# A fused linear-attention and soft-MoE kernel: loads cut into 256 KB pieces with a limit on what is under way, and a new written-out order

## The chip, the cores and the metric

The kernel runs on one core of a Trainium2 chip. Five engines have queues of their own: TensorE (PE, with its weight loads as PEld), VectorE (DVE), ScalarE (ACT), GpSimd (POOL) and SyncE (SP), which here only issues DMAs. The metric is the device time of one execution in microseconds (us), as the median of several runs.

## The reference, cut to what matters

```
# gated linear attention, 4 batches x 8 heads, 768 positions, 48 channels
scale = min(|a|, 0.999) / (|a| + 1e-6);  a = a * scale           # complex a = a_re + i a_im
for t in range(768):                                             # S: 48 x 48 per head
    S_re, S_im = a_t * (S_re + i S_im) + k_t v_t^T (real part only)
    y_t = q_t . S_re
x = y as 3072 tokens x 384
# soft mixture of experts, 8 experts x 4 slots
logits = x @ phi;  d = softmax over tokens;  c = softmax over slots
slot_out[e] = relu((d^T x)[e] @ w1[e]) @ w2[e]                   # w1, w2: 12.6 MB each
out = c @ slot_out
```

## The kernel before, in words

The recurrence is turned into 128-position blocks. Work is cut into units u = 0 to 6 of up to four (batch, block) pairs; unit 0 and unit 6 hold two pairs. For each unit the gates `ar`, `ai` (real and imaginary part, 768 KB each for a whole unit) are loaded, turned into the logarithm of the size (`gates`, tasks `g`) and into a phase (`arctan`, tasks `t`); TensorE sums them along the block (`phase`, tasks `p`, tile `up`; `logs`, tasks `e`, tile `lp`); sines and cosines (`wave`, `w`) and exponentials scale q and k (`mults`, `h`). The third part of the channels is moved inside SBUF by DMAs into the tile `hm` (`mixed`, `M`). Then for each pair come the scores (`c`, tile `qd`), the transposes (`x`), the state update (`D`), the attention output (`a`) and its transpose (`f`), and for each finished block the soft-MoE running sums (`l`, `s`). After the last block the slots are merged (`me`, `si`), the hidden layer (`hd`, `tn`), the second layer (`ex`) and the outputs (`er`, `ou`, `mi`) follow.

What runs when is written out by hand. Every task is a Python generator; the string `ORDER` names the tasks, and each word runs one task up to its next `yield`. A star on a word sets `moe.other`, which moves that step to the other engine that can do it (ACT instead of DVE, POOL instead of DVE, and so on). `_InOrder.pin` fixes the order so traced on every engine. For tasks whose names begin with `la`, `q`, `v` or `w_` (the loads of gates, q and k, v, and weights) it also makes each DMA wait for the last TensorE instruction traced so far:

```python
HELD = ("la", "q", "v", "w_")
if held and isinstance(ins, mybir.InstDMACopy) and pe in self.last:
    self.after(ins, self.last[pe])
```

All DMAs go out on SP's queue, in the order of `ORDER`, so a DMA that waits holds up all that are behind it. The weights of the two layers come in 24 pieces `w_0` to `w_23` of 1 MB (128 x 2048 floats). Pieces 0 to 4 have tiles of their own (`wx`) and may be loaded at any time; the others take over tiles that the attention part has finished with (`hm`, `vt`, `we`, `qe2`, `wf`, `q01`, `e01`, and `wx` again). The tiles `ar`, `ai` have one buffer each, so the gates of the next unit are loaded when the last use of this unit's is over. Warm-up matmuls (`zz`) keep TensorE busy where the order expects it to be idle. At the end each of the 18 output tiles is copied out of PSUM by ACT or DVE (`result`) and stored by a DMA from SP. A check of the value ranges (`gd`) ends in a branch to a slow fallback, which is not taken here.

Of the kernel before, what the change touches and what calls it, by code (L numbers as in the profile page):

```python
# [11 lines left out]
F32 = mybir.dt.float32  # L12
# [31 lines left out]
HELD = ("la", "q", "v", "w_")  # L44

# [36 lines left out]
class _Moe:  # L82
# [219 lines left out]
    L0 g0 g0 g1 g0 g1 g0* q1.1 g1 g0 g1 g1 g0 g1 g0 g1 g0 g1 T0 t0 e0.2 e0.0 e0.2 e0.0 t1 L1 e0.2 e0.1 e0.2 e0.0 la1 h0.2 p0.1  # L302
    p0.1* p0.0 e0.0 p0.2 la1 p0.2 p0.1 e0.1* k0 w_3 v1 p0.0* w_0 p0.2 p0.0 w0.2* e0.1 k0 g2 g2 e0.1 T1 w0.2 h0.0 w0.0 w0.0 zz6 zz5
    k0 g2* zz14 zz13 w0.2 zz3 g2* h0.1 h0.2 M0 k0* h0.2 w0.0 h0.1 h0.0 t2 zz10 p1.2 M0 L2 g2 h0.0 w_2 zz9 g2 p1.2 p1.0 p1.1 p1.2
    h0.1 q1.2 p1.0 zz0 p1.1 c0.0 g2 g2 p1.0 w1.2* p1.1 e1.2 e1.2 c0.0* T2 w1.2 q1.0 w1.2 e1.0 e1.0 w1.0 e1.1 la2 L3 e1.2 e1.2 e1.1
    a0.0 e1.0 e1.0 a0.0 la2 h1.2 x0.0 c0.1 e1.1 x0.0 e1.1 x0.0 zz4 h1.0 h1.2 x0.1 h1.1 M1 x0.1* q2.0 c0.1* g3 g3 T3 w1.0 a0.1
    h1.2* f0.0 w1.0 x0.1* zz12 zz1 g3* k1 a0.1* k1 f0.0 h1.0 M1 g3 k1* h1.1 t3 h1.0 q2.1 f0.1 D0.1 D0.0 p2.2 L4 g3 p2.2 h1.1 D0.0*
    w_1 q2.2 c0.2 D0.1 f0.1 g3 p2.0 c0.2 p2.2 g3 p2.0* w2.2 p2.1 T4 w2.2 v2 c0.3 a0.2 g3 p2.1* w2.2 c0.3 e2.2 p2.0 e2.2 e2.1 L5
    e2.2 e2.0 e2.2 a0.2* la3 p2.1 a0.3 f0.2 e2.1 w2.0 e2.0 la3 h2.2 e2.1 e2.1 a0.3 h2.1 e2.0 f0.2* h2.2 x0.2 x0.2* c1.0 c1.0* e2.0
    x0.2 l0 g4 g4 h2.2* l0 f0.3 f0.3 D0.2 T5 w2.0 w2.0 l0 a1.0 h2.0 l0 x0.3 x0.3 c1.1 M2 g4* D0.2 x1.0 M2 a1.0* x0.3 k2 f1.0 c1.1*  # L310
    k2 x1.0 D0.3 h2.1* g4 a1.1 x1.0* f1.0 k2* x1.1 h2.0 h2.0 t4 a1.1 D0.3* h2.1* q3.0 x1.1* q3.2 p3.2 p3.2* p3.0 x1.1* L6 g4 D1.0
# [27 lines left out]
class _InOrder:  # L339


    def __init__(self, tc):
        self.tc, self.last = tc, {}
# [11 lines left out]

    def pin(self, held=False):
# [182 lines left out]
def _polar(ctx, tc, cst, phi_sb, bad, aa, qk, vv, phi, w1, w2, consts, out):  # L539
# [44 lines left out]

    def load_a(u):
# [393 lines left out]
    er = {}  # L979
# [195 lines left out]
```

## Time and profile before

| | |
|---|---|
| median of 3 runs | 269.23 us (268.44 to 271.13) |
| the profiled execution's own time | 268.24 us |
| its span in the trace | 266.7 us |
| busy: PE, DVE, ACT, POOL | 226.7, 192.0, 185.2, 69.1 us |
| mean share of the 16 DMA engines on SP's queue | 65.3% |
| granted TensorE clock, mean | 0.963 of full speed |

Busy time is summed over a whole span with unlike stages, so it is read by stretch: in the first some 50 us the first units are prepared, then TensorE works nearly without a gap through the attention, and from about 200 us on the weights stream in beside the merge and the two layers. The profiled execution is 1 us below the median of the runs.

### The profile page before, as it was taken

Reading aid. Unit: us, or ns where it says so; the run is one execution under the profiler, and the core shown is the slowest. Engines: PE = TensorE matmul, PEld = TensorE weight load, DVE = VectorE, ACT = ScalarE, POOL = GpSimd, SP = SyncE. Lnnn points to the kernel's source line nnn. Section 1 sums busy time; section 2 is a strip of 40 time slices with the busy share of each in tenths; the row PEclk is TensorE's granted clock in tenths of the full one; section 3 lists DMA queues with packets and bytes.
Section 4 is the critical chain, followed back from the end, with each engine's and each line's share of the span. In section 5 each row is a group of like instructions: output and inputs, shape, how many; then the busy total and the mean of one; then the engine's idle time right before and its main releaser. Section 6 shows DMA issues by size and latency. Waiting matters only on the chain.

```text
span 266.7 us, 10855 instructions
## 1 busy us (share of the span) xinstructions
PE 226.7 (85%) x4828; PEld 180.5 (68%) x4828; DVE 192.0 (72%) x341; ACT 185.2 (69%) x293; POOL 69.1 (26%) x89
## 2 busy tenths in 40 slices
PE   0572976699969999999997999999969897999980
PEld 0431865588848998799885998888867663249640
DVE  4479679799938899798998898976461146575660
ACT  4979598999867898997886989698932232234230
POOL 0000004212562218512663043534830121000000
PEclk9998699989979999999999999999998999999997
DMA  6788748945830828355365565448769397979886
GB/s 172 263 300 369 236 137 298 273 167 199 294 104 7 290 77 305 85 179 223 120 200 132 201 222 161 128 132 310 265 193 366 129 413 284 375 285 394 341 297 215
DMA packets 16389, 60.95 MB, mean 228 GB/s; under 512 B 1872, under 2 KB 5200, under 8 KB 13264
## 3 DMA queue, kind: packets, MB, share of 16 engines
q1 hardware_dynamic: 16336, 60.18, 65.3%
q8 instruction: 40, 0.66, 1.0%
q14 instruction: 13, 0.11, 0.1%
HBM read 49.17 MB, written 4.72 MB: 202 GB/s over the span
## 4 chain that ended last, share of the span: by engine, by line
PE 63%; ACT 10%; DVE 9%; DMA 8%; issue 6%; POOL 1%; SPq 0%; DVEq 0%; ACTq 0%
PE qd L834 10%; PE qd L884 7%; PE up L712 7%; PE qd L890 6%; DMA ai<-in_aa_dram 5%; PE op L257 4%; PE db L863 4%; PE hp L227 4%; PE lp L712 4%; PE tp L819 3%; PE xp L898 3%; DVE ai L662 2%; PE up L710 2%; PE o L293 2%; DMA ar<-in_aa_dram 1%
## 5 line engine op out<-in xcount | busy, mean ns | idle before, releaser
L712 PE MATMUL lp<-cst,ar 128*128 128x128 f32 x144 | 20.9, 290 | 11.5 <-DVE ar L677 11.5
L712 PEld LDWEIGHTS lp<-cst,ar 128*128 128x128 f32 x144 | 20.0, 203 | 12.5 <-DVE ar L677 12.0
L884 PE MATMUL qd<-scT,vt 128*48 128x128 f32 x352 | 24.6, 283 | 2.1 <-DVE scT L846 2.0
L712 PE MATMUL up<-cst,ai 128*128 128x128 f32 x144 | 23.3, 312 | 2.2 <-ACT ai L682 1.9
L712 PEld LDWEIGHTS up<-cst,ai 128*128 128x128 f32 x144 | 22.5, 226 | 3.9 <-ACT ai L682 2.4
L846 DVE TENSOR_TENSOR scT<-qd,cst 128x1024 f32<-128x1024 f32 x16 | 19.4, 1215 | 5.9 <-ACT yT L103 4.5
L834 PE MATMUL qd<-e 32*128 32x128 f32 x384 | 22.8, 298 | 0.0
L884 PEld LDWEIGHTS qd<-scT,vt 128*48 128x48 f32 x352 | 18.8, 125 | 5.7 <-DVE scT L846 2.9
L834 PE MATMUL qd<-q 32*128 32x128 f32 x416 | 21.4, 276 | 1.3 <-issue 1.3
L729 POOL COPY cr<-fc 128x4 f32<-128x4 f32 x15 | 4.2, 283 | 67.1 <-DVE fc L727 66.9
L779 POOL TENSOR_TENSOR qe<-qe,fc 128x512 f32<-128x512 f32 (+1 forms) x14 | 17.3, 1261 | 15.6 <-DVE qe L781 10.7
L576 ACT ACT_TABLE_LOAD x15 | 19.2, 1283 | 1.3 <-PEq L1158 1.0
L834 PEld LDWEIGHTS qd<-e 32*128 32x128 f32 x384 | 16.1, 188 | 3.9 <-issue 2.4
L834 PE MATMUL qd<-hm 32*128 32x128 f32 x352 | 18.1, 273 | 0.4 <-issue 0.4
L834 PEld LDWEIGHTS qd<-q 32*128 32x128 f32 x416 | 17.0, 189 | 1.8 <-issue 1.6
L579 ACT ACT_TABLE_LOAD x14 | 18.0, 1283 | 0.3
L849 POOL TENSOR_SCALAR_AFFINE_SELECT scT<-scT 128x1024 f32<-128x1024 f32 x8 | 8.8, 1098 | 35.4 <-ACT scT L848 35.4
L898 PE MATMUL xp<-cst,yT 128*128 128x128 f32 x96 | 15.0, 283 | 2.4 <-DVE yT L105 2.2
L662 DVE TENSOR_TENSOR ai<-ai,gt 128x384 f32<-128x384 f32 x22 | 13.2, 659 | 5.1 <-DMA ai<-in_aa_dram 3.9
L779 POOL TENSOR_TENSOR q<-q,fc 128x512 f32<-128x512 f32 (+1 forms) x12 | 14.5, 1228 | 9.2 <-DVE e L781 5.8
L103 ACT COPY yT<-qd 128x512 f32<-128x512 f32 x13 | 7.7, 591 | 12.8 <-PE qd L890 10.2
L863 PE MATMUL db<-vt,kt 128*32 128x48 f32 x960 | 13.9, 211 | 1.7 <-DVE tk L105 1.7
(199 smaller groups left out, 612.3 us busy)
## 6 DMA issues: line engine op xcount, KB each, us to landing
wx<-in_w_dram SPq DMA_DIRECT2D x10, 1024.0 KB, 6.4
q<-in_qk_dram SPq DMA_DIRECT2D x10, 512.0 KB, 5.6
hm<-qe SPq DMA_DIRECT2D x20, 256.0 KB, 4.7
ar<-in_aa_dram SPq DMA_DIRECT2D x5, 768.0 KB, 4.3
ai<-in_aa_dram SPq DMA_DIRECT2D x5, 768.0 KB, 6.6
vt<-in_vv_dram SPq DMA_DIRECT2D x5, 768.0 KB, 5.7
hm<-in_w_dram SPq DMA_DIRECT2D x3, 1024.0 KB, 6.9
we<-in_w_dram SPq DMA_DIRECT2D x3, 1024.0 KB, 5.5
```

The costliest lines, as they stand in the source:

```text
L227: self.nc.tensor.matmul(out=hp[x][32 * g : 32 * g + 32, :], lhsT=zs[hi][:, c, g, :], rhs=w1_chunk(12 * hi + 4 * c + g)[:, x * 512 : (x + 1 ...
L576: ACT.preload_act_table_set(LNEXP)
L579: ACT.preload_act_table_set(TRIG)
L662: (DVE if moe.other else POOL).tensor_tensor(out=i[:, b], in0=i[:, b], in1=t[:, b], op=ALU.mult)
L712: PE.matmul(out=out[:, b], lhsT=gate[:, b, P * j : P * j + P], rhs=tri, start=not u, stop=not u or b == b1 - 1)
L779: POOL.tensor_tensor(out=out[:, w], in0=in0[:, w], in1=in1[:, w], op=ALU.mult)
L834: PE.matmul(out=qd[:, i, P * g : P * g + P], lhsT=feat(u, g, c, 1, b)[r], rhs=feat(u, g, c, 0, b)[r], start=c == 0, stop=c == 2,)
L846: DVE.tensor_tensor(out=t, in0=sc, in1=mask.unsqueeze(1).unsqueeze(1).broadcast_to([P, 4, 2, P]), op=ALU.mult)
L863: PE.matmul(out=db[o, 3 * g + c], lhsT=kt[u, b][:, g, c, o], rhs=vt[u][:, b - _span(u)[0], 4 * g + i], start=True, stop=True)
L884: PE.matmul(out=o(g, i), lhsT=vt[u][:, b - _span(u)[0], 4 * g + i], rhs=scT[u, b][:, i, g], start=True, stop=not s)
L890: PE.matmul(out=o(g, i), lhsT=st[s - 1, b][r, 3 * g + c], rhs=feat(u, g, c, 0, b)[r], start=False, stop=c == 2)
L898: PE.transpose(out=xp[:, i].rearrange("p g d -> p (g d)"), in_=yT[s, b][:, i], identity=ident)
```

## The change

Loads that are issued before the 13th weight piece in the order are cut into column pieces of at most 256 KB (`PIECE`), by the function `load`. Each such load then also waits, on SP, for an earlier load to have landed, so that the bytes of itself and of those before it that may still be under way come to no more than 1.3 MB (`paced`); the DMAs of `mixed` count too. The first DMA above 512 KB (the first of the weight pieces 12 to 23 in the order, which stay whole) switches this off for good. `ORDER` is replaced as a whole: the same tasks in another sequence, with other stars. Two loads of weights stand in the early part instead of three, and they are `w_1` and `w_2`. Of the last third of the outputs, a tile that ACT copies is stored by a DMA from ACT's queue instead of SP's. The range check `gd`, which was over before the last outputs, is moved in among them. The rest of the diff splits tile creation from use (`third`) and drops an unused second definition.

```diff
+PIECE = 1 << 18
+UNDER_WAY = 1300000
+PACED = 12
...
-    def result(self, er, sr, n, os_, out):
+    def result(self, er, sr, n, os_, out, last=False):
...
-        self.copy(out=t, in_=o, by_act=n % 2 == 1)
+        by_act = n % 2 == 1
+        act = by_act != self.other
+        self.copy(out=t, in_=o, by_act=by_act)
         yield "mi2"
-        self.store.dma_start(out=out[:, n], in_=t)
+        (nc.scalar if act and last else self.store).dma_start(out=out[:, n], in_=t)
...
-    p0.1* p0.0 e0.0 p0.2 la1 p0.2 p0.1 e0.1* k0 w_3 v1 p0.0* w_0 p0.2 p0.0 w0.2* e0.1 k0 g2 g2 e0.1 T1 w0.2 h0.0 w0.0 w0.0 zz6 zz5
+    e0.0 e0.1 p0.2 p0.0 p0.0 h0.0* p0.2* g2 g2 p0.1* p0.2 w0.2 p0.0 h0.2 la1 w_1 e0.1 T1 w0.2 w0.2 p0.1 w0.0 k0 q1.0 w_2 w0.0 w0.0
...
-    ou2 bh mi2.0 mi2.5 mi2.0 mi2.0 mi2.1 mi2.3 mi2.5 mi2.2 mi2.3* mi2.3 mi2.2 mi2.1 mi2.4 mi2.1 mi2.5 mi2.4 mi2.4 mi2.2
+    mi2.2* mi2.2 mi2.4* mi2.5 mi2.4 mi2.3 mi2.1* zz7 gd mi2.3 mi2.5* gd mi2.1 mi2.5 gd mi2.0 gd mi2.0* mi2.0
...
+    def paced(self, ins):
+
+        size = n = 4 * math.prod(c for _, c in ins.outs[0].ap)
+        if self.sent is None or size > 2 * PIECE:
+            self.sent = None
+            return
+        for s, name in reversed(self.sent):
+            n += s
+            if n > UNDER_WAY:
+                self.after(ins, name)
+                break
+        self.sent.append((size, ins.name))
...
+            if isinstance(ins, mybir.InstDMACopy) and ins.engine == self.tc.nc.sync.engine:
+                self.paced(ins)
...
+    def load(out, in_):
+        if len(out.shape) == 4 and 4 * math.prod(out.shape) > PIECE:
+            for w in range(out.shape[1]):
+                load(out[:, w], in_[:, w])
+            return
+        if 4 * math.prod(out.shape) <= PIECE:
+            SP.dma_start(out=out, in_=in_)
+            return
+        if len(out.shape) == 3:
+            out, in_ = out.rearrange("p b x -> p (b x)"), in_.rearrange("p b x -> p (b x)")
+        n = out.shape[1]
+        w = -(-n // -(-4 * P * n // PIECE))
+        for x in range(0, n, w):
+            SP.dma_start(out=out[:, x : min(x + w, n)], in_=in_[:, x : min(x + w, n)])
...
-        SP.dma_start(out=wsl[x], in_=w1[x] if x < NW1 else w2[x - NW1])
+        src = w1[x] if x < NW1 else w2[x - NW1]
+        if x < PACED:
+            load(wsl[x], src)
+        else:
+            SP.dma_start(out=wsl[x], in_=src)
```

Line numbers of the changed kernel are 3 to 40 higher than those of the kernel before for the same statement.

First place: ACT, while the gates of unit 1 are prepared. The rows with `gt` and `ar` are the steps of `gates` (the last one, on `ar`, is the exponential whose result the sums `lp` wait for), those with `n` belong to `phase`. Before:

```order
L682 ACTIVATE ai<-ai 128x1536
L576 ACT_TABLE_LOAD
L671 ACTIVATE gt<-gt 128x1536
L724 ACTIVATE n<-up 128x512 x3
L675 ACTIVATE gt,esum<-ar 128x1536
L741 ACTIVATE fc_284<-fc_284 128x512
L579 ACT_TABLE_LOAD
L745 ACTIVATE fc_284<-fc_284 128x512
```

The same place in the changed kernel:

```order
L715 ACTIVATE ai<-ai 128x1536
L596 ACT_TABLE_LOAD
L704 ACTIVATE gt<-gt 128x1536
L757 ACTIVATE n<-up 128x512
L708 ACTIVATE gt,esum<-ar 128x1536
L757 ACTIVATE n<-up 128x512 x2
L599 ACT_TABLE_LOAD
L778 ACTIVATE fc_275<-fc_275 128x512
```

The exponential has moved ahead of the second and third `n`, and the absolute value on ACT (`fc`, line 741 before) has gone to DVE.

Second place: SP, from the gates of unit 1 to those of unit 2 (`wx` is a weight piece, `hm` the copies inside SBUF of unit 0). Before:

```order
L610 DMA q_131<-in_qk_dram 128x1024
L589 DMA ar<-in_aa_dram 128x1536
L591 DMA ai<-in_aa_dram 128x1536
L969 DMA wx<-in_w_dram 128x2048
L620 DMA vt<-in_vv_dram 128x1536
L969 DMA wx<-in_w_dram 128x2048
L806 DMA hm<-qe_114 64x2x256 x4
L969 DMA wx<-in_w_dram 128x2048
L610 DMA qe_288<-in_qk_dram 128x1024
L610 DMA q_131<-in_qk_dram 128x1024
L589 DMA ar<-in_aa_dram 128x1536
```

The same stretch in the changed kernel:

```order
L611 DMA q_129<-in_qk_dram 128x512 x2
L618 DMA ar<-in_aa_dram 128x512 x3
L618 DMA ai<-in_aa_dram 128x512 x3
L618 DMA wx<-in_w_dram 128x512 x4
L611 DMA q_129<-in_qk_dram 128x512 x2
L618 DMA wx<-in_w_dram 128x512 x4
L839 DMA hm<-qe_114 64x2x256 x4
L618 DMA vt<-in_vv_dram 128x512 x3
L611 DMA qe_312<-in_qk_dram 128x512 x2
L618 DMA ar<-in_aa_dram 128x512 x3
```

Ahead of the `hm` copies stand two weight pieces and half a load of q and k, now in ten pieces; a third weight piece behind them is gone, and v has moved behind the copies.

Third place: DVE in unit 5, where the four products of `ai` (task `g6`) and the copy of the carry `tk` (task `k4`) stand. Before:

```order
L781 TENSOR_TENSOR qe_1613<-qe_1613,fc_1718 128x1024
L662 TENSOR_TENSOR ai<-ai,gt 128x384 x4
L105 COPY tk<-ctp 128x128
L846 TENSOR_TENSOR scT<-qd,cst 128x1024
L867 TENSOR_TENSOR st<-db,st 128x288
```

On ACT in the changed kernel, where the copy of `tk` is now (the row with `tsum` is the step that reads the products of `ai`):

```order
L106 COPY d<-mt 128x128
L106 COPY xs<-xp 128x4x2x48
L106 COPY yT<-qd 128x512
L106 COPY tk<-ctp 128x128
L702 ACTIVATE gt,tsum<-ai 128x1536
```

The copy of `tk` no longer stands behind the four products of `ai` in its queue.

## Rows read from the trace of the kernel before

**Rows 1.** Busy time by stretch, with granted clock, DMA share and rate.

```profile
core 0: us, PE busy (x) PEld busy (x) DVE busy (x) ACT busy (x) POOL busy (x), PEclk, DMA share, GB/s
10.00:54.00 44.00, 31.20 (x348) 23.94 (x349) 33.30 (x59) 37.78 (x53) 5.14 (x9) 0.90 0.75 257
54.00:200.00 146.00, 139.15 (x3454) 120.46 (x3455) 122.03 (x179) 122.14 (x186) 60.14 (x71) 0.98 0.56 182
```

**Rows 2.** What PE waited for, 54 to 200 us: total, times, longest.

```profile
PE qd L890 <- issue: 2.5, 1, 2.5
PE tp L819 <- DVE q L781: 2.0, 1, 2.0
PE db L863 <- DVE tk L105: 1.7, 1, 1.7
```

**Rows 3.** Timeline, 20 to 40 us: start, duration, instruction [idle before, releaser].

```profile
28.62 1.76 DVE L673 SCALAR_TENSOR_TENSOR ar<-ar,gt 128x1536 f32<-128x1536 f32 x1 [0.48 <-ACT gt L671]
...
32.62 0.60 ACT L724 ACTIVATE n<-up 128x512 f32<-128x512 f32 x1 [1.08 <-PE up L712]
...
32.95 0.50 PE L834 MATMUL qd<-e 32*128 32x128 f32 x8
33.11 1.48 ACT L675 ACTIVATE gt<-ar 128x1536 f32<-128x1536 f32 x1
...
34.16 0.40 PE L834 MATMUL qd<-hm 32*128 32x128 f32 x8
...
34.71 1.76 DVE L677 SCALAR_TENSOR_TENSOR ar<-ar,gt 128x1536 f32<-128x1536 f32 x1 [3.14 <-ACT gt L675]
...
36.53 1.16 PE L712 MATMUL lp<-cst,ar 128*128 128x128 f32 x8 [1.64 <-DVE ar L677]
```

**Rows 4.** Timeline of DMA issues on SP, 12 to 30 us.

```profile
13.13 0.33 SPq L589 DMA_DIRECT2D ar<-in_aa_dram  x1
...
25.50 2.70 SPq L806 DMA_DIRECT2D hm<-qe  x4
```

**Rows 5.** DMA issues: count, KB each, us from issue to landing.

```profile
ar<-in_aa_dram SPq DMA_DIRECT2D x1, 768.0 KB, 4.3
ai<-in_aa_dram SPq DMA_DIRECT2D x1, 768.0 KB, 4.5
...
hm<-qe SPq DMA_DIRECT2D x4, 128.0 KB, 2.4
...
out_dram<-vt SPq DMA_DIRECT2D x3, 256.0 KB, 3.0
...
wx<-in_w_dram SPq DMA_DIRECT2D x10, 1024.0 KB, 6.4
```

**Rows 6.** SP's DMA queue, 224 to 248 us and 259 to 264 us: packets, MB, busy share.

```profile
q1 hardware_dynamic: 1104, 8.12, 89.0%
...
q1 hardware_dynamic: 864, 1.56, 86.0%
```

**Rows 7.** The gates of unit 2: chain of waits, then timeline of DVE and PE.

```profile
41.00 7.53 DMA ai<-in_aa_dram
...
48.62 1.96 DVE L662 TENSOR_TENSOR ai<-ai,gt 128x384 f32<-128x384 f32 x4 [1.71 <-DMA ai<-in_aa_dram]
...
51.33 0.63 PE L898 MATMUL xp<-cst,yT 128*128 128x128 f32 x4 [2.25 <-DVE yT L105]
```

**Rows 8.** Timeline of DVE, unit 5.

```profile
140.39 3.24 DVE L662 TENSOR_TENSOR ai<-ai,gt 128x384 f32<-128x384 f32 x4 [0.80 <-DMA ai<-in_aa_dram]
```

**Rows 9.** Timeline: a step of the range check, then the last copy and stores.

```profile
237.88 0.55 DVE L1055 TENSOR_REDUCE good<-xs 128x1 f32<-128x384 f32 x1
...
259.82 0.68 DVE L105 COPY wf<-o 128x512 f32<-128x512 f32 x1
260.22 1.81 SPq L298 DMA_DIRECT2D out_dram<-wf  x2
262.08 0.60 SPq L298 DMA_DIRECT2D out_dram<-we  x1
```

More of the change, by code (lines that the diff above doesn't have):

```diff
@@ L304 @@
[L304 to L311, printed above, removed]
@@ new lines @@
+    w_4 zz14 g3* a0.1 zz3 f0.0 zz12 w_0 q2.2 a0.1* zz1 zz4 k1 g3 h1.0 k1 D0.1 t3 k1* f0.1 D0.0 h1.1 h1.0 p2.2 h1.1 L4 g3 f0.1
+    D0.0* D0.1 c0.2 p2.1 g3 q2.1 p2.2 c0.2 p2.0 g3 p2.2 p2.1* c0.3 w2.2 g3 a0.2 T4 w2.2 w2.2 c0.3 p2.0* e2.2 p2.1 a0.2* e2.2 e2.1
+    p2.0 e2.1 e2.0 w2.0 L5 e2.2 e2.2 la3 e2.0 a0.3 e2.1 h2.2 x0.2 e2.1 h2.2 e2.0 x0.2 e2.0 la3 x0.2 c1.0 h2.1 k2 f0.2 D0.2 a0.3
+    c1.0* D0.2 f0.3 f0.3 f0.2* x0.3 l0 x0.3* k2 c1.1 l0 h2.2* M2 g4 g4 l0 x0.3* h2.0 T5 w2.0 a1.0 g4* w2.0 D0.3 h2.1* k2 a1.0 l0*
@@ new lines @@
+    g4 c1.1* x1.0 D0.3 x1.0* h2.0 h2.0 M2 h2.1* x1.0 f1.0 a1.1 D1.0 f1.0* t4 v2 D1.0 a1.1 x1.1 x1.1* p3.2 p3.2* p3.2 x1.1 l0 q3.0
+    w3.2 q3.2 p3.0 L6 g4 D1.1 s0 p3.0 g4 c1.2 c1.2 v3 q3.1 p3.1 g4 p3.0 c1.3 T6 w3.2 a1.2 p3.1* w3.2 g4 D1.1 p3.1 e3.2 e3.2 L7
+    e3.2 s0 e3.0 c1.3* e3.1 e3.2 la4 a1.2 e3.1* w3.0 e3.0 la4 x1.3 h3.2 e3.0 a1.3 x1.3* e3.0 x1.3* e3.1 e3.1 h3.2 f1.1 h3.0 a1.3
+    x2.0 f1.1* k3 x2.0 x1.2 x2.0 x1.2* c2.0 x1.2* g5 g5 T7 w3.0 w3.0 c2.0* D1.2 k3 D1.2 h3.2* h3.1 g5* f1.2 c2.1 k3 s0 a2.0 l1
@@ new lines @@
+    er3 er2 tn0* tn0 er1 er3 er2 ex0 hd w_19 gd ex0 ex1 er4 w_20 hd ex0 tn1 er1 tn1 tn1* er3 er0 ex0 tn1* er5 er0 er1 ex1 ex0 ex1
+    ex0 ex1 er2 ex0 w_23 ex1 ex0 ou0 er1 ex1 ex1 er0 ou0 mi0.0 mi0.1 mi0.3 mi0.0* er5 mi0.4 ex2 er5 mi0.1* mi0.3* ex1 mi0.0 ou1
+    mi0.4 er5 mi0.1 mi0.3 mi0.4 ex2 ex2 ou1 mi0.5 mi1.2 mi0.2 mi1.4 ex2 mi0.5 mi0.5 mi1.2* mi1.2 mi1.1 ex2 mi1.3 mi1.4* mi0.2
+    mi1.5 mi0.2 mi1.1* mi1.3* mi1.5* mi1.1 mi1.4 ex2 ex2 ex2 mi1.3 mi1.0 mi1.5 ou2 ou2 mi1.0* bh mi2.2 mi1.0 mi2.1 mi2.4 mi2.3
@@ L342, in __init__ @@
     def __init__(self, tc):
-        self.tc, self.last = tc, {}
+        self.tc, self.last, self.sent = tc, {}, []
         self.traced = tc.nc.cur_bb.bb.instructions
@@ L588, in load_a, with third @@
         b0, b1 = _span(u)
-        SP.dma_start(out=ar[u][:, b0:b1], in_=aa[u, 0][:, b0:b1])
+        load(ar[u][:, b0:b1], aa[u, 0][:, b0:b1])
         yield "la1"
-        SP.dma_start(out=ai[u][:, b0:b1], in_=aa[u, 1][:, b0:b1])
+        load(ai[u][:, b0:b1], aa[u, 1][:, b0:b1])
     qe = {}
+    def third(u):
+        if (u, 2) not in qe:
+            qe[u, 2] = wk.tile([P, 2, 2, UB, P], F32, name="qe2", bufs=1)
+        return qe[u, 2]
     def load_qk(u, j):
@@ L597, in load_qk @@
         if j == 2:
-            t = qe[u, 2] = wk.tile([P, 2, 2, UB, P], F32, name="qe2", bufs=1)
-            qs = t[:, 0]
+            qs = third(u)[:, 0]
         else:
@@ L609, in load_qk @@
         h0, h1 = (b0, b1) if j == 2 else _held(u)
-        SP.dma_start(out=qs[:, :, h0:h1], in_=qk[u][:, j, :, b0:b1])
+        load(qs[:, :, h0:h1], qk[u][:, j, :, b0:b1])
     def load_v(u):
@@ L619, in load_v @@
         vt[u] = t.rearrange("p (b h d) -> p b h d", h=H, d=D)
-        SP.dma_start(out=vt[u][:, h0:h1].rearrange("p b h d -> p b (h d)"), in_=vv[u][:, b0:b1])
+        load(vt[u][:, h0:h1].rearrange("p b h d -> p b (h d)"), vv[u][:, b0:b1])
     def last_e():
@@ L642, in _polar @@
     wsl = {}
-    def load_w(x):
-        pool, name = place[x % len(place)]()
-        kw = dict(bufs=1) if name == "qe2" else {}
-        wsl[x] = pool.tile([P, WC], F32, name=name, **kw)
-        SP.dma_start(out=wsl[x], in_=w1[x] if x < NW1 else w2[x - NW1])
     def gates(x):
@@ L756, in logs @@
         if j == 2:
-            e = hc_[u, j] = qe[u, 2][:, 1]
+            e = hc_[u, j] = third(u)[:, 1]
         else:
@@ L968, in load_w @@
         wsl[x] = pool.tile([P, WC], F32, name=name, **kw)
-        SP.dma_start(out=wsl[x], in_=w1[x] if x < NW1 else w2[x - NW1])
+        src = w1[x] if x < NW1 else w2[x - NW1]
[3 more added lines that the diff above has]
+            SP.dma_start(out=wsl[x], in_=src)
     def swap():
@@ L1040, in result @@
     def result(x, n):
-        yield from moe.result(er, sums_of(x), n, lambda: os_tile(x, n), out[x])
+        yield from moe.result(er, sums_of(x), n, lambda: os_tile(x, n), out[x], x == NX - 1)
     good = ys.tile([P, 6], F32, name="good", bufs=1)
```

44 lines of the change are left out of this document (20 added, 24 removed).

## The prediction

> **What bounds the kernel now.** I read first the busy time by stretch, then what TensorE waited for, then the timeline and the DMA issues around each wait. From 54 to 200 us TensorE works 139.15 of 146.00 us [rows 1]: this stretch is bound by it, and 6.85 us are left to win there. Three waits make up nearly all of that: 2.5 us that no engine ended ("issue"), 2.0 us for a product on DVE, and 1.7 us for the copy of `tk` on DVE [rows 2]. From 10 to 54 us it works 31.20 of 44.00 us [rows 1], so 12.8 us are idle, with ACT at 37.78 of 44.00: here the first units pass through chains of ACT and DVE steps, and the order of these steps and the landing of the gates decide. DMA engines are busy 0.75 of that stretch and 0.56 of the next [rows 1], so bytes bound neither; a single late load can.
>
> All times below are of the profiled execution (268.24 us; span 266.7). The median of the runs is 269.23, 0.99 above it, and I put the sum of the differences on the median.
>
> **The early order: -2.0 us.** Before, the exponential on `ar` starts at 33.11, directly behind the `n` that waited for TensorE's `up` and ran from 32.62 [rows 3]. Its input was finished by DVE at 28.62 + 1.76 = 30.38 [rows 3]. In the new order it stands before the second and third `n`, so it can start at 30.4 and end at 31.9; DVE's last step (34.71, 1.76 [rows 3]) then waits for nothing else and ends near 33.7. TensorE has the scores in front of the sums `lp`; they run from 32.95 to 34.16 + 0.40 = 34.56 [rows 3]. So `lp` can start at 34.5 instead of 36.53 [rows 3], 2.0 us earlier, and what is late next is TensorE itself. ACT gains as much: its second and third `n` now fall into time in which it waited. Bounds: 0, if the gates of unit 2 are what ends the stretch whatever comes before; -4.3, if besides TensorE's wait of 2.25 us at 51.33 [rows 7] goes (the larger gain, below). The middle, 2.0, is worked out step by step and I take it.
>
> **The pieces: +0.3 us.** A load of 1 MB takes four issues on SP instead of one, 0.33 us each [rows 4]; SP only issues DMAs, and after a load it mostly waits for TensorE's place in the order, so this hides behind that wait. A row of 8 KB (the weights) costs 0.89 x 16 x 24 / 1104 = 0.31 us of one engine for 8.12 MB / 1104 = 7.36 KB, 23.8 GB/s; a row of 2 KB (the stores at the end) 0.86 x 16 x 5 / 864 = 0.080 us for 1.81 KB, 22.7 GB/s [rows 6]. So 2 KB rows cost 5%, 0.1 us on a load of 768 KB. Loads of gates are on the path in two places (waits of 1.71 and 0.80 us on DVE [rows 7, 8]); 0.1 us each, and 0.1 for the added waits of ACT and DVE on three landings instead of one. Bounds 0 (a piece used before the others have landed pays it back) and +1.0.
>
> The Trainium skill's page "DMA: Bandwidth & Descriptors", section "Rules for kernel authors", speaks against this edit: it wants at least 1 MiB per DMA for full bandwidth. The rows of this trace put the loss from row size at 5% when enough DMAs are under way; by that rule the time would be that of the slower rival below.
>
> **The limit: 0 us, if a piece lands in 4.6 us or less.** A piece of 256 KB waits until it and its elders are at most 1.3 MB: itself and three others make 1.05 MB, a fifth 1.31 MB, so four are under way. With a landing time L one piece goes out every L/4. The critical queue is SP's early one: `w_1`, half of q, `w_2` are ten pieces ahead of the `hm` copies. The first may go when the gates `ar` have landed, 13.13 + 4.3 = 17.4 [rows 4, 5]; the tenth at 17.4 + 9 L/4. The copies need 2.70 us of issues [rows 4] and 2.4 to land [rows 5], and the scores that read them start at 32.95, so they must go out by 27.85: L up to 4.6 us. Nearest rows for L: 128 KB alone 2.4, 256 KB stores 3.0, 768 KB alone 4.3, whole weights 6.4 [rows 5]. I take 3.0, the same size: tenth piece at 24.2, copies when DVE has made them, 25.50 as before [rows 4]. That the limit speeds the gates up by keeping weights out of their way I do not expect: with three large loads issued close behind it, `ai` of unit 1 landed in 4.5 us, hardly more than `ar` alone in 4.3 [rows 5].
>
> **The middle: -1.5 us.** TensorE's wait of 1.7 us in unit 5 is for `tk` [rows 2], which stood on DVE behind the four products of `ai`: these began 0.80 us late for their load and took 3.24 us [rows 8]. With the copy on ACT ahead of them the 1.7 goes. DVE is busy 122.03 of 146.00 us [rows 1], so another of its results is late soon after; I count -1.0. The 2.0 us for a product on DVE [rows 2] lie where unit 6 had its products on POOL and DVE and now has fewer on POOL; I can't follow which step is late next and count -0.5, bounds -2.0 and +1.0. The 2.5 us of "issue" [rows 2] I leave where they are. A new order can make waits of its own in 146 us; +2.0 is the bound for that, the size of one wait like these.
>
> **The tail: 0 us.** SP issued the last three stores from 260.22 to 262.68, though the last copy ended at 260.50 [rows 9]. With four of six issues on ACT up to 1.6 us could go. Against that, the last output now stands behind the range check; two or three steps like the one of 0.55 us [rows 9] and a small matmul cost up to 1.5. The Trainium skill (same page, section "Issuing engines are not separate DMA queues") says a second issuing queue saves the issue time alone; by that the gain is at most these 1.6 us, which is how I bound it.
>
> **Sum:** -2.0 + 0.3 + 0 - 1.5 + 0 = -3.2; 269.23 - 3.2 = **266.0 us**, with its own range 263.5 to 268.
>
> **Rivals.** *Nothing comes of it.* TensorE's stretch from 54 us is full, and what is gained early is lost at the gates of unit 2: their `ai` took 7.53 us from 41.00 and held DVE 1.71 us [rows 7]. If that load stays as slow and starts no earlier, the early term is 0 and the middle's -1.5 stands against a new wait: 269.23 + 0.3 - 0.5 = 269.0. For it: ACT and DVE are nearly full there. Against: q is now loaded earlier, so fewer bytes stand around that load.
>
> *Larger gain.* The gates of unit 2 land in 4.5 us as those of unit 1 did [rows 5] instead of 7.53 [rows 7], because copies and loads that came behind them are held until they are nearly done. 3.0 us less on the load take away the 2.25 us that TensorE then waited [rows 7], and with DVE free earlier another 1.2 in the middle: 266.0 - 3.5 = 262.5.
>
> *Slower.* The limit of four pieces starves the queue. If L is nearer to 6.4 than to 3.0, the tenth piece goes out at 17.4 + 14.4 = 31.8, the `hm` copies land at 36.9, the scores of unit 0 (1.6 us) end at 38.5 and `lp` starts there, 2.0 us later than before. Loads of gates in three pieces then take 2.8 us longer than 4.3 (6.4 and two issues), once on the path: 269.23 + 2.0 + 2.8 + 0.3 - 1.8 (what is left of the middle and the tail) = 272.5. It decides from L = 4.6 on. For it: whole weights do take 6.4 us [rows 5], and 256 KB pieces queue behind each other. Against: with four under way there is little to queue behind. It is also the direction of the rule on 1 MiB that the Trainium skill gives.
>
> **How the numbers follow.** Forecast 0.40, larger gain 0.15, nothing 0.23, slower 0.22. A measurement of this kernel can tell about 1%, 2.7 us: 266.5 and 271.9 are the borders. Of the forecast about 0.26 lies below 266.5; with all of the larger gain and 0.04 of "nothing", faster is 0.45. Slower is the last rival, 0.22. The rest, 0.33, is within 1%. The range runs from 262.0 to 272.0: below it lies a part of the larger gain, above it rather more than half of the slower rival.
>
> **What would show it.** In the trace after: `lp` of unit 1 near 34.5 us; pieces of 256 KB landing in about 3 us; the early `hm` copies out by 26 us; no wait of TensorE for `tk` in unit 5; TensorE idle about 10 us, not 12.8, between 10 and 54 us. I am wrong if pieces land in over 4.6 us, if SP then holds up `hm` or gates, if new waits on DVE of over 1.5 us stand in the middle, or if the last store goes out later after the last matmul than before.

## The result, and the profile after

The changed kernel takes 260.72 us (median of 4 runs, 259.17 to 264.08) against 269.32 us beside it: ratio 0.9645, interval 0.956 to 0.9729. Two later series of six runs of the unaltered kernel gave 262.32 and 260.82 us against 268.40 and 268.94 us. Single runs of the changed kernel spread by 4 to 6 us, those of the kernel before by 3 to 13, so differences below 2 us are read from the traces. Ratios and their intervals leave out runs more than 1.5% above the fastest of their kernel, so in the series of the exponential and the 64 matmuls one unusually quick run of the kernel before (264.80 us) draws them to 1, and medians of all runs stand beside them. The profiled execution took 262.23 us, with a span of 260.7 us against 266.7 us before.

The forecast, 266.0 us, had the direction, but the time lies below its range, which began at 262.0; the gain came out at two to nearly three times its size (8.6, 6.1 and 8.1 us in the three series, against 3.2).

By stretch, as in [rows 1] (columns as there):

```profile
10.00:54.00 44.00, 30.72 (x359) 23.38 (x360) 34.57 (x61) 37.51 (x52) 6.59 (x11) 0.92 0.78 244
54.00:200.00 146.00, 140.78 (x3550) 120.55 (x3550) 120.66 (x185) 122.61 (x188) 51.83 (x61) 1.00 0.62 191
```

TensorE is idle no less between 10 and 54 us (13.3 us against 12.8). But from 54 to 200 us its granted clock is 1.00, not 0.98: the stretch has no low clock left in this trace. What TensorE waited for there, as in [rows 2]:

```profile
PE db L896 <- issue: 1.9, 1, 1.9
PE tp L852 <- issue: 0.8, 1, 0.8
PE up L743 <- DVE st L900: 0.8, 1, 0.8
PE up L745 <- issue: 0.6, 1, 0.6
```

The three long waits of [rows 2] are gone, and `issue` now stands elsewhere. The early step, as in [rows 3] (timeline: start, duration, instruction, wait):

```profile
28.14 1.76 DVE L706 SCALAR_TENSOR_TENSOR ar<-ar,gt 128x1536 f32<-128x1536 f32 x1 [0.61 <-ACT gt L704]
...
29.93 1.48 ACT L708 ACTIVATE gt<-ar 128x1536 f32<-128x1536 f32 x1 [1.34 <-DVE ar L706]
...
31.41 1.07 ACT L757 ACTIVATE n<-up 128x512 f32<-128x512 f32 x2
31.54 1.76 DVE L710 SCALAR_TENSOR_TENSOR ar<-ar,gt 128x1536 f32<-128x1536 f32 x1 [0.44 <-ACT gt L708]
...
33.91 1.05 PE L745 MATMUL lp<-cst,ar 128*128 128x128 f32 x8
```

The exponential stands ahead of two `n`; DVE's step waits 0.44 us instead of 3.14, and `lp` starts at 33.9 instead of 36.53. Landings, as in [rows 5], and the issue of the early copies, as in [rows 4]:

```profile
wx<-in_w_dram SPq DMA_DIRECT2D x20, 256.0 KB, 4.3
hm<-qe SPq DMA_DIRECT2D x20, 256.0 KB, 4.0
...
ar<-in_aa_dram SPq DMA_DIRECT2D x15, 256.0 KB, 3.1
ai<-in_aa_dram SPq DMA_DIRECT2D x15, 256.0 KB, 4.0
```

```profile
25.67 3.59 SPq L839 DMA_DIRECT2D hm<-qe  x4
```

By these medians a piece lands in 3.1 to 4.3 us, not in the 3.0 that I took, but under the 4.6 from which the slower rival decides (the weight pieces ahead of the early copies took 3.9 to 4.4); the copies go out at 25.67.

To see where the time was gained I weighed each matmul by the usual duration of its shape, left the warm-ups out, and read from both traces when a share of that work from 27 us on was done (worked out from the PE timelines; another run of the changed kernel beside it). The two orders do the work in another sequence, so an entry moves by 1 us, beside a wait by 2, with the weights chosen; the steps stay:

```
share of TensorE's work   before    after  difference   second trace of after
 5%                        42.33    39.64    -2.7            -1.9
15%                        69.8     68.2     -1.7            -2.4
20%                        83.8     78.7     -5.1            -6.2
25%                        93.0     89.5     -3.5            -4.9
50%                       140.7    136.8     -3.9            -4.1
75%                       192.0    191.3     -0.8            -1.5
80%                       205.7    201.5     -4.1            -5.0
95%                       246.1    239.3     -6.8            -7.1
100%                      259.4    254.2     -5.2            -5.4
```

So the early 2 us are there. Two more steps come between 15 and 25% and between 75 and 80%, 2.4 us more by 95%; 3 us are lost between 50 and 75%, and 1.6 at the end.

### The profile page after: what moved, and what is told of

The parts are those of the page before. It is cut to its first block, busy times and chain, and to the rows that moved or that the text cites. A ratio compares the mean times of both kernels' runs of the same rounds, so it can differ in the third digit from the quotient of the medians.

```text
span 260.7 us, 10985 instructions
## 1 busy us (share of the span) xinstructions
PE 223.1 (86%) x4828; PEld 177.1 (68%) x4828; DVE 189.5 (73%) x342; ACT 187.3 (72%) x296; POOL 62.3 (24%) x81
## 4 chain that ended last, share of the span: by engine, by line
PE 67%; DMA 12%; DVE 9%; ACT 5%; issue 3%; SPq 1%; DVEq 0%
PE qd L867 12%; PE qd L917 7%; PE qd L923 7%; PE lp L745 6%; PE up L745 5%; PE tp L852 4%; PE hp L230 4%; PE op L260 4%; DMA wx<-in_w_dram 4%; PE db L896 3%; DMA hm<-qe 3%; DMA ar<-in_aa_dram 3%; PE xp L931 2%; PE lg L115 2%; DVE scT L879 2%
## 5 line engine op out<-in xcount | busy, mean ns | idle before, releaser
L879 DVE TENSOR_TENSOR scT<-qd,cst 128x1024 f32<-128x1024 f32 x16 | 19.5, 1221 | 11.9 <-ACT yT L106 7.4
L917 PE MATMUL qd<-scT,vt 128*48 128x128 f32 x352 | 23.8, 277 | 2.0 <-DVE scT L879 1.7
L745 PEld LDWEIGHTS up<-cst,ai 128*128 128x128 f32 x144 | 21.2, 213 | 4.4 <-ACT ai L715 1.7
L745 PE MATMUL up<-cst,ai 128*128 128x128 f32 x144 | 21.9, 297 | 2.6 <-ACT ai L715 1.4
L106 ACT COPY yT<-qd 128x512 f32<-128x512 f32 x18 | 10.6, 592 | 16.9 <-PE qd L923 9.7
L917 PEld LDWEIGHTS qd<-scT,vt 128*48 128x48 f32 x352 | 18.2, 122 | 6.4 <-DVE scT L879 2.7
L896 PEld LDWEIGHTS db<-vt,kt 128*32 128x32 f32 x960 | 11.9, 110 | 6.6 <-issue 3.6
L814 DVE TENSOR_TENSOR q<-q,fc 128x1024 f32<-128x1024 f32 (+1 forms) x13 | 14.6, 1140 | 0.2
L867 PEld LDWEIGHTS qd<-hm 32*128 32x128 f32 x352 | 14.6, 187 | 0.0
L812 POOL TENSOR_TENSOR qe<-qe,fc 128x512 f32<-128x512 f32 x8 | 11.9, 1506 | 9.7 <-DMA ar<-in_aa_dram 5.1
```

Source lines behind the costliest of these rows:

```text
L106: self.nc.scalar.copy(out=out, in_=in_)
L745: PE.matmul(out=out[:, b], lhsT=gate[:, b, P * j : P * j + P], rhs=tri, start=not u, stop=not u or b == b1 - 1)
L812: POOL.tensor_tensor(out=out[:, w], in0=in0[:, w], in1=in1[:, w], op=ALU.mult)
L814: DVE.tensor_tensor(out=out, in0=in0, in1=in1, op=ALU.mult)
L867: PE.matmul(out=qd[:, i, P * g : P * g + P], lhsT=feat(u, g, c, 1, b)[r], rhs=feat(u, g, c, 0, b)[r], start=c == 0, stop=c == 2,)
L879: DVE.tensor_tensor(out=t, in0=sc, in1=mask.unsqueeze(1).unsqueeze(1).broadcast_to([P, 4, 2, P]), op=ALU.mult)
```

## The experiments

Each time is the median of six runs (twelve in one case), beside the kernel before on the same chip.

My theory after the result: the order made the gain (theory O), by the early step and by waits that went in the middle, with the low clock behind them. Rivals: the pieces and the limit made it (theory P); or the order pays only with the pieces (theory J).

### Order without pieces, and pieces without the order

Whole loads, no limit, new order:

```diff
-PIECE = 1 << 18
-UNDER_WAY = 1300000
+PIECE = 1 << 30
+UNDER_WAY = 1 << 40
```

> The changed kernel with every load whole and no limit; the new order and the stores from ACT stay. Theory O (the order makes the gain, by its removed waits and by the clock that stays up where TensorE doesn't wait): 260 to 262 us, the early `lp` of unit 1 near 34 us. Theory P (pieces and limit make it, because loads land sooner): 266 to 269 us. If the order fits only loads of this size (theory J): over 264 us, with new waits on loads.

261.30 us against 268.34, ratio 0.9766 (0.9703 to 0.9828); `lp` of unit 1 at 34.1 us. All of the gain is there without pieces.

Pieces and limit with the old order (`ORDER` of the kernel before in the changed kernel):

> The changed kernel with the order of the kernel before: pieces, limit and stores from ACT stay. Theory O: 268.5 to 270.5 us. Theory P: 261 to 264 us. Theory J: 269 us or more, since the old order was laid out for whole loads.

267.20 us against 268.34, ratio 0.9841 (0.9753 to 0.993), between the two theories, and by the median nearer to O. Its six runs lie between 262.42 and 268.77 us, and the ratio rests on the two lowest; so the times don't rule out that pieces, limit and second queue give a part. Its trace, of the longest run, is no faster than that of the kernel before: `lp` of unit 1 starts at 37.2 us, 0.7 later, and the span is 267.0 us.

Pieces without the limit:

```diff
-UNDER_WAY = 1300000
+UNDER_WAY = 1 << 40
```

> The changed kernel with pieces but no limit on the bytes under way. If the limit only orders what the queue does anyway (my term of 0): 260 to 261.5 us. If it keeps weights out of the way of gates and copies: `ai` of unit 2 lands later than the 4.0 us of the changed kernel, by 2 us or more, and the time is 262.5 us or more. If the limit starves the queue: 258 to 259.5 us.

265.61 us, ratio 0.9798 (0.97 to 0.9895), 3 to 5 us over the changed kernel. In its trace half of `ai` of unit 1 is late by 0.94 us on DVE, `lp` starts at 34.8, and weight pieces land in 6.0 us between 8 and 56 us; `ai` of unit 2 takes 6.9 us from its first issue to its last landing, 6.5 in the changed kernel. By the medians pieces without a limit are 4 us worse than whole loads, but the intervals of the two ratios overlap. If the difference is real, the limit only takes back what the pieces cost.

What pieces cost shows in the rate. Pieces in the changed kernel from 17 to 20 us (packets, then SP's queue: packets, MB, share of 16 engines):

```profile
DMA packets 528, 0.96 MB, mean 321 GB/s; under 512 B 58, under 2 KB 58, under 8 KB 528
## 3 DMA queue, kind: packets, MB, share of 16 engines
q1 hardware_dynamic: 528, 0.96, 92.6%
```

Whole loads in the kernel before from 17 to 24 us:

```profile
DMA packets 453, 2.83 MB, mean 404 GB/s; under 512 B 47, under 2 KB 47, under 8 KB 291
## 3 DMA queue, kind: packets, MB, share of 16 engines
q1 hardware_dynamic: 453, 2.83, 98.5%
```

An engine moves 0.96 MB / (0.926 x 16 x 3 us) = 21.6 KB per us in pieces and 25.7 whole: 16% less, where I had 5%; with the four-piece limit the queue also idles more, 321 GB/s against 404. The Trainium skill, page "DMA: Bandwidth & Descriptors", section "Rules for kernel authors", asks for at least 1 MiB per DMA; these two rates agree with its direction.

### Stores, and the unaltered kernel again

All stores on SP's queue:

```diff
-        (nc.scalar if act and last else self.store).dma_start(out=out[:, n], in_=t)
+        self.store.dma_start(out=out[:, n], in_=t)
```

> The changed kernel with all stores on SP's queue. My term for the tail was 0 with bounds -1.6 to +1.5. If the second queue gives back the issue time of the last stores: 261.3 to 262.3 us. If the end is set by the landing of the last store and what follows it: 260 to 261 us, as the changed kernel.

263.15 us, ratio 0.9754 (0.9675 to 0.9833). From the last step on `xs` to the end of the span it took 262.1 - 249.39 = 12.7 us, against 11.0, 11.9 and 11.4 in three traces of the changed kernel. The second queue gives back 0.8 to 1.7 us, which is about the issue time that I had as its bound (1.6). The Trainium skill, same page, section "Issuing engines are not separate DMA queues", says that a second issuing engine saves the time of issuing alone; these spans agree.

> The changed kernel once more, unaltered, to put it beside the others on the same chip and to see which of its stalls come back. Order theory and clock theory alike: 259 to 264 us. The wait of 1.9 us that the first trace put at `issue` (TensorE, 140 us) should be elsewhere or gone if it is chance, in the same place if the order makes it.

262.32 us, ratio 0.9788 (0.9732 to 0.9844). The `issue` wait came back at the same instruction with the same length; first trace, then this one:

```profile
140.22 0.88 PE L896 MATMUL db<-vt,kt 128*32 128x48 f32 x61 [1.87 <-issue]
```

```profile
139.98 0.88 PE L896 MATMUL db<-vt,kt 128*32 128x48 f32 x61 [1.87 <-issue]
```

So the place isn't chance. But the program alone doesn't make the wait: with all stores on SP TensorE's program is the same up to there, and its trace shows these matmuls without one:

```profile
137.58 1.24 PE L896 MATMUL db<-vt,kt 128*32 128x48 f32 x96
```

### Half of each order

The new order up to the word L5 (57 us) and the old one behind it, each word of a task that has run left out, and the reverse; all else as in the changed kernel.

> The changed kernel with its new order up to the word L5 (about 57 us), and from there the order of the kernel before. If the gain is made early (the exponential moved ahead, loads of q earlier) and kept: 262 to 264 us. If the early gain is only 1.5 to 2.5 us, as the curve of work done says at 60 to 70 us, and the rest is made behind it: 265 to 267 us. If the early gain is lost at the next waits: 268 us.

272.27 us, ratio 1.0162 (1.0108 to 1.0216): outside every expectation. The early gain is there (`lp` at 33.6, 2.3 us ahead until 69 us), but then the loads of the gates of unit 3, in pieces behind those of v, come late. ACT, then TensorE, in the timeline:

```profile
76.63 1.48 ACT L689 ACTIVATE ar<-ar 128x1536 f32<-128x1536 f32 x1 [9.72 <-DMA ar<-in_aa_dram]
...
82.04 0.47 PE L852 MATMUL tp<-cst,e 128*128 128x128 f32 x1 [7.35 <-DVE st L108]
```

> The changed kernel with the order of the kernel before up to the word L5, and from there the new one. The mirror of the run before: if the gain is made early and kept, 267 to 268 us; if most of it is made behind 57 us, 262.5 to 265 us; if early and late parts only work together, over 268 us.

268.54 us (twelve runs), ratio 1.002 (0.9985 to 1.0055). It has no early gain, and waits of 2.20 us for `tk` (80.76) and of 2.58 for the copies of unit 6 (203.82) of its own. The halves don't add up: where an order is cut, a new wait comes, so this pair says only that neither half alone keeps the gain.

### The clock

Before, the granted clock falls to half behind three waits, at 52, 76 and 198 us, besides a stretch from some 24 to 32 us that both kernels have (0.57 and 0.58). Extra warm-ups in the first and the last of these waits, in the kernel before:

```diff
+    at("zy0", warm, 8, True)      # word ahead of the first f0.1
+    at("zy1", warm, 7)            # word ahead of the first x4.3
```

> The kernel before with extra warm-up matmuls in two of TensorE's waits, eight ahead of the transpose that waits at 51.33 us and seven ahead of the one that waits at 198.26 us; nothing else is changed, and the waits for DVE stay. Clock theory (each wait of 2 us or more drops the granted clock to half for some 3.5 us, which costs 1.6 us): the clock stays at 1.00 at 52 to 56 and 198 to 204 us, and the time falls by 2.5 to 3.3 us, to 265 to 266 us. If the low clock costs nothing on the path, or falls all the same: 267.5 to 269.5 us.

275.48 us against 268.40, ratio 1.0251 (1.0193 to 1.031): slower by 7 us, and both theories missed. Busy time and clock of TensorE in this run, then in the kernel before:

```profile
52.00:54.00 2.00, 1.25 (x50) 1.00 0.36 121
54.00:56.00 2.00, 2.00 (x47) 1.00 0.15 33
```

```profile
52.00:54.00 2.00, 2.00 (x98) 0.61 0.45 150
54.00:56.00 2.00, 2.00 (x13) 0.54 0.02 6
```

In the first place the clock stayed up, and yet at 15% of the work the run is only 0.1 us ahead: TensorE comes earlier to its next wait, 0.86 us for ACT at 57.36. The low clock there lay beside work of ACT and DVE that sets the pace. In this trace (of the longest of the six runs, 278.17 us) most was lost around the last place, where the clock fell all the same (0.69 from 200 to 204 us). This run, then the kernel before with DVE's product ahead of its wait:

```profile
200.13 0.49 PE L834 MATMUL qd<-hm 32*128 32x128 f32 x4 [3.55 <-issue]
...
201.04 2.73 PE L877 MATMUL zz<-idb 128*128 128x512 bf16 x7
```

```profile
197.05 0.68 DVE L781 TENSOR_TENSOR q<-q,fc 128x512 f32<-128x512 f32 x1
...
198.26 0.27 PE L819 MATMUL tp<-cst,e 128*128 128x128 f32 x1 [2.03 <-DVE q L781]
```

The wait now came ahead of the seven warm-ups, put at `issue`, and these then took 2.73 us of their own. And in the kernel before, DVE's product was done at 197.73, 0.5 us before TensorE went on: the wait that the profile puts to DVE ended with something else. The next section shows with what. A further wait at `issue`, 1.26 us at 210.37 before, is 1.96 us here, again with a low clock behind it. The rule in my clock theory doesn't hold either: behind a wait of 2.04 us at 46.49 in the kernel before the clock was 1.00.

### The blocks of TensorE's program

The profile has a queue of its own for instructions. Kernel before, page, then the answers for 73.8 to 74.0 and 77.4 to 77.6 us, and the wait between:

```profile
q8 instruction: 40, 0.66, 1.0%
...
q8 instruction: 1, 0.02, 32.9%
...
q8 instruction: 1, 0.02, 34.8%
```

```profile
73.27 0.42 PE L890 MATMUL qd<-q,st 32*48 32x128 f32 x16
73.49 0.40 PE L890 MATMUL qd<-hm,st 32*48 32x128 f32 x7
...
76.39 0.68 PE L890 MATMUL qd<-hm,st 32*48 32x128 f32 x9 [2.50 <-issue]
```

These are 40 packets of 0.66 MB / 40 = 16.5 KB, or 68 bytes for each of the 9,656 matmuls and weight loads that the page counts on TensorE; that they are TensorE's program is inferred from this and from what follows. A packet passes at 73.8, the wait ends 2.5 us later, the next packet passes 1.1 us behind that. The same 2.4 to 2.7 us stand ahead of the ends at 210.37 (before), 140.22 (after) and 200.13 (with warm-ups). With the eight warm-ups ahead of it the wait at 76 us came eight matmuls earlier in the stream, after 31 of 48 instead of 39:

```profile
73.22 0.42 PE L893 MATMUL qd<-q,st 32*48 32x128 f32 x15
75.80 0.27 PE L893 MATMUL qd<-q,st 32*48 32x128 f32 x1 [2.16 <-issue]
```

So the wait belongs to a place in the count of instructions, not to an operation. The traces bear this out: counted over TensorE's records (9,730 in the kernel before), all 48 of its waits at `issue` of over 0.3 us, in 17 traces, end 193 or 194 instructions behind a multiple of 256; a packet of 16,384 bytes, by this, is 256 instructions of 64 bytes. Five more waits end there that the profile puts to DVE or a DMA, 0.2 to 0.9 us after these were done; the one at 198.26 us before is among them. Not every such border has a wait (the 140 us one came in three traces of the changed kernel, and in no other trace with the same program up to there). If the place is set by the count, instructions put ahead of everything must move the wait in the work. 64 tiny matmuls (32 x 32 on 8 columns, of zeros) in the first 9.8 us, in which TensorE has nothing to do:

```diff
+        for _ in range(PAD):       # PAD = 64, the first word of ORDER
+            PE.matmul(out=tp[0:32, 0, 0:8], lhsT=nop, rhs=nop[:, 0:8], start=True, stop=True)
```

In the kernel before:

> The kernel before with 64 tiny matmuls (and their weight loads, 128 instructions) ahead of everything on TensorE, in the 9.8 us in which it has nothing to do. Block theory (TensorE's own program arrives in blocks of 16.4 KB, no closer than some 3.5 us, and the waits put at `issue` are for these blocks): the wait of 2.5 us at 76 us moves or falls below 1 us, the low clock behind it (76 to 80 us) goes too, other waits of this kind may come elsewhere; 264 to 266.5 us if none comes. Chance theory (the wait is a matter of what the DMA engines do at that time): it stays at the same place and the time is 267.5 to 269.5 us.

The wait at 76 us is gone, and the low clock with it (TensorE, 76 to 80 us; the kernel before had 0.58 and 0.56):

```profile
76.00:78.00 2.00, 2.00 (x53) 1.00 0.35 121
78.00:80.00 2.00, 1.86 (x62) 1.00 0.04 8
```

From 15 to 20% of the work it gains 3.9 us, to 25% still 2.5. But the time is 269.03 us against 269.78 (ratio 1.0074, 0.9983 to 1.0165): waits of this kind now take 1.21, 1.85, 0.80 and 1.45 us (at 148, 194, 207 and 218 us; the second and third at the borders of 198 and 210 us before, 64 matmuls earlier in the work), and the gain is gone by 85%. In the changed kernel:

> The changed kernel with the same 64 tiny matmuls at the start. Block theory: the wait of 1.87 us at 140 us, which stood in both traces of this kernel, is gone from there; waits of this kind in all may be smaller or larger than 3.3 us, so 259.5 to 265 us. Chance theory: it stays near 140 us, 261 to 263 us.

The wait at 140 us is gone; others of 0.87 and 1.68 us came, at 166 and 243 us. The time, 267.27 us against 269.78 (ratio 0.9994, 0.9892 to 1.0097), is 5 us over the changed kernel and misses both expectations. It had lost 3 to 4 us by 60 us already, with waits of 2.13 and 1.70 us where the changed kernel has 1.50 and 2.02 (for DVE and ACT, not for blocks), and then the clock at half; why is open:

```profile
44.00:52.00 8.00, 4.46 (x97) 1.00 0.78 235
52.00:60.00 8.00, 6.30 (x109) 0.57 0.74 229
```

### The early step alone

One word of the old order moved, in the kernel before:

```diff
-    h0.1 q1.2 p1.0 zz0 p1.1 c0.0 g2 g2 p1.0
+    h0.1 q1.2 g2 p1.0 zz0 p1.1 c0.0 g2 p1.0
```

> The kernel before with one word moved: the exponential on `ar` of unit 1 ahead of the second and third `n` on ACT. My early term alone: `lp` of unit 1 starts near 34.5 us instead of 36.5. If the 2.0 us are kept to the end: 266 to 266.8 us. If they are lost at the gates of unit 2 or at the next wait (the rival that nothing comes of it): 267.8 to 268.8 us.

267.21 us against 269.78 by the medians of all runs, -2.6; the interval of the ratio, 0.9866 to 1.0093, doesn't tell it from no change. The trace does: `lp` at 33.96 us, and 2.4 to 2.5 us ahead at 10 and 15% of the work. It is kept to 80% and grows there, since the block wait at 76 us, at the same matmul, is now 0.86 us long and the clock stays up; 2 us go again behind 205 us, with a block wait of 1.68 us and a low clock:

```profile
72.19 0.44 PE L890 MATMUL qd<-hm,st 32*48 32x128 f32 x9 [0.86 <-issue]
...
205.97 0.38 PE L834 MATMUL qd<-q 32*128 32x128 f32 x3 [1.68 <-issue]
```

### The range check, whole loads, and warm-ups

The last four words `gd` moved from among the last outputs to those of the second third:

```diff
-    mi2.2* mi2.2 mi2.4* mi2.5 mi2.4 mi2.3 mi2.1* zz7 gd mi2.3 mi2.5* gd mi2.1 mi2.5 gd mi2.0 gd mi2.0* mi2.0
+    mi2.2* mi2.2 mi2.4* mi2.5 mi2.4 mi2.3 mi2.1* zz7 mi2.3 mi2.5* mi2.1 mi2.5 mi2.0 mi2.0* mi2.0
...
-    mi0.5 mi0.5 mi1.2* mi1.2 mi1.1 ex2 mi1.3 mi1.4* mi0.2 mi1.5 mi0.2 mi1.1* mi1.3* mi1.5* mi1.1 mi1.4 ex2
+    mi0.5 mi0.5 mi1.2* gd mi1.2 mi1.1 ex2 mi1.3 gd mi1.4* mi0.2 mi1.5 mi0.2 mi1.1* gd mi1.3* mi1.5* mi1.1 gd mi1.4 ex2
```

> The changed kernel with the four last steps of the range check moved from among the last outputs to the second third of the outputs. If the check holds up the end (the last output's matmul stands behind a small one that waits 1.4 us for DVE): 260.8 to 261.5 us, about 1.2 us less than the changed kernel, and the last copy starts 1 to 1.4 us sooner behind the last hidden-layer result. If the last stores' landing sets the end whatever stands there: as the changed kernel, 262 to 262.6 us.

261.47 us against 269.78, ratio 0.9788 (0.9698 to 0.9879). From the last `xs` to the end 9.9 us instead of 11.0 to 11.9, about 1 us as expected. A new wait ate it: the copies of unit 6 (`e<-qe`) stood on SP behind eight paced pieces of weights.

```profile
183.00 8.29 SPq L618 DMA_DIRECT2D we<-in_w_dram  x8
191.35 2.63 SPq L839 DMA_DIRECT2D e<-qe  x4
```

```profile
198.64 0.81 PE L867 MATMUL qd<-e 32*128 32x128 f32 x8 [3.94 <-DMA e<-qe]
```

The changed kernel issues them at 192.48 us, as late; there they landed in 3.4 us by the median, here in 5.9. Then the unaltered kernel, whole loads with the early check, and no warm-ups from 41 to 48 us, on one chip:

> The changed kernel, unaltered, as the mark for the two runs beside it: 260 to 263 us.

260.82 us against 268.94, ratio 0.9718 (0.9637 to 0.98). The block wait at 141 us is there for the third time, 1.61 us.

> The changed kernel with the range check early and every load whole, with no limit. If pieces and limit give nothing with this order (theory O) and the check costs about 1 us at the end: 260 to 261.5 us, a little under the changed kernel. If pieces with a limit do help behind the early part: 262.5 us or more.

(The edits are those of the whole loads and of the early check, above.)

258.31 us (256.05 to 260.07), ratio 0.9646 (0.9557 to 0.9735): better than expected, 2.5 us under the changed kernel and the lowest median of all, though the two intervals overlap. The copies of unit 6 now stand behind two whole loads and go out 8 us earlier, and no block waits at 140 us:

```profile
178.94 3.09 SPq L611 DMA_DIRECT2D we<-in_w_dram  x2
183.03 3.11 SPq L839 DMA_DIRECT2D e<-qe  x4
```

Ten tiny matmuls at the start, and no warm-ups between 41 and 48 us:

```diff
-    w_4 zz14 g3* a0.1 zz3 f0.0 zz12 w_0 q2.2 a0.1* zz1 zz4 k1
+    w_4 g3* a0.1 f0.0 w_0 q2.2 a0.1* k1
```

> The changed kernel without its five warm-up matmul pairs between 41 and 48 us; ten tiny matmuls at the start keep the instruction blocks of what follows where they were. Clock theory: the clock falls to half for 3 to 7 us between 46 and 58 us, and the time is 263.5 to 266 us, 1.5 to 3.5 us over the changed kernel. If a low clock there is covered by the waits for ACT and DVE, as the run with warm-ups in the old order suggests: within 1 us of the changed kernel.

263.86 us (259.95 to 265.64), 3 us over its neighbour by the medians; the ratios, 0.977 (0.9648 to 0.9893) and 0.9718, don't part them. The clock did fall:

```profile
44.00:50.00 6.00, 4.33 (x101) 0.61 0.91 261
50.00:56.00 6.00, 4.88 (x85) 0.53 0.85 273
```

At 10% of the work it is 0.4, 1.4 and -0.2 us behind the three traces of the changed kernel (the last with a low clock of its own from 46 to 50 us), and at 15% 0.5, 1.2 and -0.2, though it ran near half the clock for over 10 us. In this trace most of it was covered, as it was with the warm-ups in the old order. What the six runs lost is open. The blocks were kept in place (0.54 us at 188.12, at the matmul at which the changed kernel waits 0.81 us at 190.82), and still no wait came at 140 us.

## Why the prediction was wrong

**The early order (-2.0): right.** 2.6 us at `lp` (2.3 and 1.4 in two more traces), 1.7 to 2.4 at 15% of the work, and the word alone gives 2.4. It isn't lost at the gates of unit 2, so the rival that nothing comes of it falls.

**The middle (-1.5), and the waits at `issue` that I put at nothing: this is the step that failed.** I wrote "The 2.5 us of `issue` I leave where they are". They don't stay: they are a wait for a block of TensorE's own program, whose place is fixed in the count of instructions, and a new order puts other instructions there. With the low clock behind it the wait cost 3.9 us up to 20% of the work, 1.8 to 2.5 of it kept to 25%; the run with 64 matmuls ahead shows both. The wait at 198 us I took, with the profile, for a wait for DVE's q, and had it at -0.5; it stands at a border too, and its last 0.5 us are the block's. Without it and the low clock from 198 to 204 us, 3.4 us are gained from 75 to 80%. The wait for `tk` (-1.0) went as I said, but a block wait of 1.87 us came at the same `db` matmuls; with two more of 0.6 and 0.8 us, 2.6 to 3.1 us are lost again from 50 to 75%. In all, from 15 to 80%: -2.5, a term of about the right size made of parts most of which were wrong; that the sum came near is luck.

**Behind 200 us I had no term** but the tail, and 2.1 to 2.7 us are gained there up to 95%. A block wait of 1.26 us at 210.37 before is part of it, the same kind of wait again; the rest I can't tell apart. Between the two traces the gain is 6.0 us where I had 3.2: 0.9 more in the middle, some 2.4 behind 200 us, and the tail below takes part of it back. How far the time lies below the range is chance: the second series, 262.32 us, is inside it. And part of the gain hangs on more than the order: with 64 matmuls ahead, the same order is 5 us slower; what I could trace of that lies in waits for DVE and ACT, and its cause is open.

**The pieces (+0.3): priced too low per engine,** 16% less and not 5%. In the time of the whole kernel it doesn't show: with this order whole loads are as good (261.3), or perhaps better (258.3 with the check early).

**The limit (0): right in the place that I looked at, missed in another.** The early copies go out in time. But at 183 us eight paced pieces hold SP for 8.3 us ahead of the copies of unit 6, and TensorE waited 2.1, 2.6 and 3.9 us for these in three variants. It is the mechanism of my slower rival, at the other end of the kernel. The larger gain was not that rival's either: a piece of `ai` of unit 2 landed in 4.4 to 4.9 us, but the whole took 6.5 us from the first issue to the last landing (38.60 to 45.05; 5.5 in the second trace), as long as with whole loads in this order and not the 4.5 that the rival needs, and the stretch from 10 to 54 us lost no idle time by it.

**The tail (0): +1.3 to +2.2 us** from the last `xs` to the end (9.7 before; 11.0, 11.9 and 11.4 after). The second queue gives back 0.8 to 1.7, the late check costs about 1 (9.9 without it in one trace, 11.0 in another with whole loads), and landings vary as much. I had priced the check's steps, not the branch behind them: in the changed kernel the last store lands at 257.52 us, but POOL, which branches at 255.32, runs its next instruction at 258.49, and SP's closing steps start behind it at 259.05; with the check early they wait for the last landing alone, at 260.05, and the span ends 1.3 us after it instead of 3.2.

## What to carry to other kernels

A wait that a profile puts at `issue` on TensorE is not fixed: look at the instruction queue beside it, count the instructions up to it, and expect a new order to move it. A wait put to an engine that had been done for 0.5 us may be one of these. Price an early step by its own wait, and try it alone: one word gave 2.4 us in its trace. Before cutting loads into paced pieces, look at every short copy that stands behind them in the same queue.

## What the runs showed that I had not expected

- TensorE's program comes in packets of 16.5 KB on a queue of its own. Around the `issue` waits of 1.8 us and more two of them lie 3.4 to 3.8 us apart (around shorter ones up to 6.3), and the wait ends 2.2 to 2.7 us behind the first. That they are fetched one ahead, and no faster, fits these rows; it wasn't measured by itself.
- 8 extra matmuls moved such a wait by exactly 8 matmuls; 64 took it away, and four came elsewhere in the work. The waits stand at every 256th instruction, but not each time at each of these.
- A granted clock near one half (1.2 GHz) for 3 to 10 us cost between next to nothing (52 to 56 us, 45 to 56 us) and 1.4 us (of the 3.9 at 76 us). Where it cost nothing, ACT or DVE set the pace. In these traces it followed waits of 1.7 to 3.9 us, but not all of them: 2.02 us in the first trace after, 2.39 in the second and 2.04 before (46.49 us) had a clock of 1.00 behind them.
